# A fifth block product as seven small ones in the first channel product of an attention and MLP-mixer kernel

## The chip, the core and the metric

The kernel runs on one core of a Trainium2 chip. Its time is the device time of one execution, in microseconds (us). Three runs of the kernel before took 822.70, 823.24 and 823.75 us; the median is 823.24 us. The profiled execution took 823.35 us, of which the trace covers a span of 821.6 us.

## What is computed

A routed attention over 4 batches and 8 heads gives x of 768 tokens by 512 channels for each batch. A token mixer and a channel mixer follow. Cut to what matters here:

```
x  = attention(q, k, v, centroids)             # (4, 768, 512)
h  = relu(x^T @ w_tok1) @ w_tok2               # token mixer
u  = x + h^T
h2 = relu(u @ w_ch1) @ w_ch2                   # channel mixer: 512 -> 1536 -> 512
out = u + h2
```

The change lies in the product `u @ w_ch1`, called the first channel product.

## The kernel before

**Seven products for eight.** The channel products are done with the seven-product scheme of Strassen in Winograd's form. Both matrices are cut into 2 by 2 blocks. The left one is w_ch1 (blocks A11 to A22, sums S1 to S4, table `left_weights`), the right one is u transposed (blocks B11 to B22 of `uT`, sums T1 to T4, made by `u_sums`). Seven block products, named in the table `SEVEN`, give the four blocks of the result. VectorE (DVE) makes the sums of the operands and adds the products up; ScalarE (ACT) copies some of them out of PSUM and takes the relu.

**Parts.** The four batches are taken in the order 0, 2, 3, 1, and each is done in three parts, 12 in all. A part is one call of `ch1_pair`, which makes a third of the hidden rows (two chunks of 128, i = 0 and 1, by twice 384 tokens), and one call of `ch2_chunks`, which multiplies them by their third of w_ch2 and adds the result onto x. For `ch2_chunks` seven combinations of the hidden rows are needed; four of them, S1 to S4, are made by DVE at the end of `ch1_pair` (`sum_1`, `sum_2`, `sums_34`). `by_turns` runs the 21 items of `ch2_chunks`: the product p1 for chunks 0, 1, 2, then p5 for 0, 1, 2, then c11, and so on. Each item is two matmuls of 128x256 and one add by DVE, and after each item `between` takes one entry from the list `late` (ends of `ch1_pair` that wait their turn) and one from the list `others` (sums of operands for later parts).

**Sets.** In 11 of the 12 parts (all but the first) `ch1_sets` is used. There the scheme is applied a second time to four of the seven block products: Y (A12 by B21), P (S1 by T1), Z (S4 by B22) and X (A22 by T4). One block product is four matmuls of 128x384 (two chunks by two halves of the contraction); as a "set" it is seven of 128x192. The other three block products (A11 by B11, S2 by T2, S3 by T3) stay as they are, four matmuls of 128x384 each. The sums of the small blocks lie in the tiles `w1ss` (weights, made once) and `uTss` (u, made for each batch by `set_right_sums`).

**What sets the order.** The program is written out by hand: every engine executes its instructions in the order in which the code issues them, and waits are put in where an operand, or a buffer that is to be written over, isn't ready. PSUM has eight banks: three under the tag X, three under Z, and two under Y (`ptile`). A bank is given out again in turn, and the first matmul of its new user waits for the last reader of its old one. In `ch1_sets` the small products that are summed into one place run as a chain through a bank: p1, u2, c22, c21 in one accumulation (`chain`), with one add by DVE after each.

**Memory.** x of batch 1 is kept in the pool `x1pool` and is written to DRAM (the tile `spill`) after the first two batches' token mixers, so that its room can be used for the sums; it is read back into the room of batch 0 when that is done.

Of the kernel before, what the change touches and what calls it, by code (L numbers as in the profile page):

```python
# [18 lines left out]
C = 16  # L19
# [31 lines left out]
def kernel(  # L51
# [49 lines left out]
    tokpool = pool("tokpool", 1, tokens)  # L101
    staging = fast.enter_context(ExitStack())
# [30 lines left out]
    spill = spilled.tile([P, NJ, DM], F32, name="spill")  # L133
    xs = [(x1pool if b == 1 else xpool).tile([P, NJ, DM], F32, name=f"x{b}") for b in range(B)]
# [466 lines left out]

    def set_lefts():
        if "l2" not in pools:
            pools["l2"] = pools["w2sums"].tile([P, 4, 3, HS], F32, name="w1ss")
        l2 = pools["l2"]
        yx = W["ch1"].rearrange("p f (i r c) -> p f i r c", i=2, r=2)[:, 2:4]
        pz = pools["w1s"][:, 0:3:2].rearrange("p i f (r c) -> p f i r c", r=2)
        for n, both in enumerate((yx, pz)):
            blocks = [both[:, f, :, r] for r in range(2) for f in range(2)]
            sums_ = [l2[:, 2 * n : 2 * n + 2, m] for m in range(3)]  # L610
            yield dict(
                zip(("A11", "A12", "A21", "A22", "S1", "S2", "S4", "S3"), blocks + sums_ + blocks[2:3])
            )
# [6 lines left out]
    def set_rights():  # L620
        uT, R, r2 = pools["uT"], pools["R"], pools["r2"]
        yz = uT[:, :, 2:4].rearrange("p n f (k t) -> p n f k t", k=2)
        x, p = (R[name].rearrange("p f (k t) -> p f k t", k=2) for name in ("T4", "T1"))
        for blocks, sums_ in (
            ([yz[:, :, f, k] for f in range(2) for k in range(2)], [r2[:, 0:2, m] for m in range(3)]),
            ([x[:, f, k] for f in range(2) for k in range(2)], [r2[:, 2, m] for m in range(3)]),
            ([p[:, f, k] for f in range(2) for k in range(2)], [r2[:, 3, m] for m in range(3)]),
        ):
            yield dict(
                zip(("B11", "B12", "B21", "B22", "T1", "T2", "T4", "T3"), blocks + sums_ + blocks[1:2])  # L630
            )

    def set_right_sums():

        pools["r2"] = pools["w2sums"].tile([P, 4, 3, HS // 2], F32, name="uTss")
        return [list(winograd_right(blocks)) for blocks in set_rights()]

    def set_blocks():

        (yx, pz), (yz, x, p) = (list(y) for y in (set_lefts(), set_rights()))  # L640
        left = {name: {k: a[:, i] for k, a in two.items()} for two, i, name in
                ((yx, 0, "Y"), (yx, 1, "X"), (pz, 0, "P"), (pz, 1, "Z"))}
        right = {"Y": {k: b[:, 0] for k, b in yz.items()}, "Z": {k: b[:, 1] for k, b in yz.items()},
                 "X": x, "P": p}
        return left, right
# [94 lines left out]
    def between(n=1):  # L740
        if late:
            late.pop(0)()
        for _ in range(min(n, len(others))):
            others.pop(0)()

    def by_turns(n, product, of, last=False, after=()):
# [10 lines left out]
        for m in range(len(order) // 2):  # L757
# [9 lines left out]
            between()  # L767
# [16 lines left out]
    def ch1_pair(part, sets, beside):  # L784
# [6 lines left out]
        p5, c12 = (pools["mlp"].tile([P, 2, HS], F32, name=k) for k in ("p5", "c12"))  # L791
# [10 lines left out]

        def big(psum, a, r, i, start):
            product(psum, a, r, i, start)
            between()
            if a != "A11" and beside:
                beside.pop(0)()
# [13 lines left out]
        def sums_34():  # L821
            nc.vector.scalar_tensor_tensor(
                out=h2["S3"], in0=c12, scalar=0.0, in1=a11, op0=ALU.max, op1=ALU.subtract
            )
            sub(h2["S4"], a12, h2["S2"])

        (ch1_sets if sets else ch1_plain)(
            part, product, big, relu, a11, a12, a22, p5, c12, sum_1, sum_2, sums_34
        )

    def ch1_plain(part, product, big, relu, a11, a12, a22, p5, c12, sum_1, sum_2, sums_34):
# [24 lines left out]
        def late_(i):  # L856
            product(X[i], "A22", "T4", i, False)
            nc.scalar.activation(out=a12[:, i], in_=X[i], func=ACT.Relu)
            (sums_34 if i else sum_2)()
# [4 lines left out]
    def ch1_sets(part, product, big, relu, a11, a12, a22, p5, c12, sum_1, sum_2, sums_34):  # L864

        left, right = set_blocks()
        n0, n1 = slice(0, HS // 2), slice(HS // 2, HS)

# [7 lines left out]
        def direct(bank, which, start=True):  # L876
            small(bank[:, n0], which, "c11", start)
            small(bank[:, n1], which, "c12", start)

        def chain(q, which, name, x):  # L880

            small(q[:, n0], which, name, name == "p1")
            src = q[:, n0]
            if len(x.shape) == 3:
                src = src.unsqueeze(1).to_broadcast([P, 2, HS // 2])
            add(x, src, x)

        def column(z, which, x):
            small(z[:, n0], which, "p5")
            add(x[:, :, n1], z[:, n0].unsqueeze(1).to_broadcast([P, 2, HS // 2]), x[:, :, n1])  # L890

        X = [ptile("X", HS), None]
        big(X[0], "A11", "B11", 0, True)
        nc.scalar.copy(out=a11[:, 0], in_=X[0])  # L894
        ybe = ptile("Y", HS)
        direct(ybe, "Y")
        add(a11[:, 0], ybe, a11[:, 0])
        X[1] = ptile("X", HS)
        big(X[1], "A11", "B11", 1, True)
        nc.scalar.copy(out=a11[:, 1], in_=X[1])  # L900
        pbe = ptile("Z", HS)
        direct(pbe, "P")
        nc.scalar.copy(out=p5[:, 0], in_=pbe)
        yq, pq = ptile("Y", HS), ptile("Z", HS)
        chain(yq, "Y", "p1", a11[:, 0, n0])
        chain(pq, "P", "p1", p5[:, 0, n0])
        big(X[0], "S2", "T2", 0, False)
        chain(yq, "Y", "u2", a11[:, 0, n1])
        yz, pz = ptile("X", HS), ptile("Z", HS)
        column(yz, "Y", a11)  # L910
        chain(pq, "P", "u2", p5[:, 0, n1])
        small(pz[:, n0], "P", "p5")
        nc.scalar.copy(out=p5[:, 1, n1], in_=pz[:, n0])
        relu(a11[:, 0])
        add(p5[:, 0, n1], pz[:, n0], p5[:, 0, n1])
        add(c12[:, 0], X[0], p5[:, 0])
        big(X[1], "S2", "T2", 1, False)
        chain(yq, "Y", "c22", a11[:, 1, n1])
        chain(pq, "P", "c22", p5[:, 1, n1])
        direct(ybe, "Z")  # L920
        chain(yq, "Y", "c21", a11[:, 1, n0])
        small(pq[:, n0], "P", "c21", False)
        nc.scalar.copy(out=p5[:, 1, n0], in_=pq[:, n0])
        relu(a11[:, 1])
        add(c12[:, 0], ybe, c12[:, 0])
        chain(yz, "Z", "p1", c12[:, 0, n0])
        add(c12[:, 1], X[1], p5[:, 1])
        big(X[0], "S3", "T3", 0, False)
        add(a22[:, 0], X[0], p5[:, 0])
        relu(a22[:, 0])  # L930
        chain(yz, "Z", "u2", c12[:, 0, n1])
        column(pbe, "Z", c12)
        big(X[1], "S3", "T3", 1, False)
        add(a22[:, 1], X[1], p5[:, 1])
        relu(a22[:, 1])
        chain(yz, "Z", "c22", c12[:, 1, n1])
        direct(X[0], "X", False)
        nc.scalar.copy(out=a12[:, 0], in_=X[0])
        small(X[1][:, n0], "X", "c21", False)
        nc.scalar.copy(out=a12[:, 1], in_=X[1])  # L940
        chain(yz, "Z", "c21", c12[:, 1, n0])
        chain(yq, "X", "p1", a12[:, 0, n0])
        sum_1()

        def late_1():
            chain(yq, "X", "u2", a12[:, 0, n1])
            column(pz, "X", a12)
            sum_2()

        def late_2():  # L950
            chain(yq, "X", "c22", a12[:, 1].rearrange("p (k t) -> p k t", k=2))
            relu(a12)
            sums_34()

        late.extend([late_1, late_2])
# [166 lines left out]
    for b in (0, 2):  # L1122
# [26 lines left out]
        if b == 2:  # L1149
            take(turning, len(turning))  # L1150
            usums = u_sums()
            tok2_chunks(b, {13: lambda: next(usums)})
        else:
# [3 lines left out]
            nc.sync.dma_start(spill, xs[1])  # L1157
# [7 lines left out]
    batches = (0, 2, 3, 1)  # L1165
    for n, b in enumerate(batches):
        turning = []
        for part in range(3):
# [8 lines left out]
            ch1_pair(part, not first, [turning.pop(0) for _ in turning[:UCOLS]])  # L1177
# [25 lines left out]
            if part == 2 and not last:  # L1203

                yz, x, p = steps
                yz[0]()
                yz[1]()
                next(usums)

                others += [lambda: next(usums)] * 2  # L1210
                others.append(lambda: [step() for step in (yz[2], p[2], yz[3], p[3])])
                others += [lambda: None, lambda: (x[0](), x[1]()), lambda: (x[2](), x[3]())]
                if n == 0:
                    xs[1] = xpool.tile([P, NJ, DM], F32, name="x0")
                    nc.sync.dma_start(xs[1], spill)
# [216 lines left out]
```

## Time and profile before

| | value | where from |
|---|---|---|
| PE busy | 814.2 us, 99% of the span | part 1 of the page |
| DVE busy | 631.1 us, 77% | part 1 |
| ACT busy | 374.7 us, 46% | part 1 |
| PE's share of the chain that ended last | 98% | part 4 |
| granted TensorE clock | 1.00 | span and clock of the core |
| from the first matmul of the first part to that of the second | 393.51 to 429.75 us | timeline of PE |
| one part with sets, 535.69 to 571.00 us | PE busy 35.31, DVE 21.87, ACT 5.56 us | busy time by stretch |
| one matmul pair of 128x384, 128x256, 128x192 | 1.29, 0.86, 0.65 us | steps of the timeline of PE |

The page gives busy time for each engine and the chain of work that ended last. The trace can also be asked for the instructions of one engine in order of time (start, duration, line, tiles, and in brackets how long the engine was idle before and what ended that). In that timeline a matmul of this kernel leaves two records, so "x4" is two matmuls; the duration of a merged row runs to the end of its last record, while the next row starts earlier, as matmuls are pipelined. The step from one row's start to the next is therefore what a group of matmuls costs.

### The profile page before, as it was taken

The numbers are of one execution on the slowest core, as the hardware profiler recorded it, in microseconds if no ns is written. First come the engines' busy times: TensorE is split into PE (matmuls) and PEld (weight loads), VectorE is DVE, ScalarE is ACT, GpSimd is POOL, SyncE is SP. The second block draws the span as 40 slices with busy tenths as digits, with TensorE's granted clock in tenths as the row PEclk, the third lists the DMA queues.
The fourth block names the chain that finished last, engine by engine and source line by source line (L and its number), as shares of the span: only waits on it lengthen the run. The fifth ranks groups of instructions, "written<-read, shape, count | busy, mean of one in ns | idle before, by whom it ended". The sixth has DMA issues, their size and how long they took to land.

```text
span 821.6 us, 11693 instructions
## 1 busy us (share of the span) xinstructions
PE 814.2 (99%) x4348; PEld 535.5 (65%) x4348; DVE 631.1 (77%) x1206; ACT 374.7 (46%) x573; POOL 30.7 (4%) x28
## 2 busy tenths in 40 slices
PE   8999999999999999999999999999999999999997
PEld 4444444444444444444588888888888888888876
DVE  6879898989898978859797788755777566775665
ACT  5588776777878776127202154121441204511120
POOL 1001010111011000000000000000000000000000
PEclk9999999999999999999999999999999999999999
DMA  8797666768676434143000025000240001400002
GB/s 156 142 162 135 140 142 122 149 139 163 130 160 137 95 104 122 51 127 79 0 1 1 5 45 183 1 0 1 38 117 0 1 1 30 125 1 1 1 0 81
DMA packets 184258, 63.41 MB, mean 77 GB/s; under 512 B 172800, under 2 KB 176896, under 8 KB 183936
## 3 DMA queue, kind: packets, MB, share of 16 engines
q1 hardware_dynamic: 182592, 62.18, 34.7%
q8 instruction: 36, 0.59, 0.3%
q10 hardware_dynamic: 1600, 0.39, 0.2%
q14 instruction: 30, 0.25, 0.1%
HBM read 36.21 MB, written 7.86 MB: 54 GB/s over the span
## 4 chain that ended last, share of the span: by engine, by line
PE 98%; DVE 1%; issue 0%; ACT 0%; DVEq 0%; ACTq 0%
PE sc L413 19%; PE av L455 15%; PE pX L966 15%; PE pX L798 12%; PE pZ L966 7%; PE ph L534 5%; PE pY L871 5%; PE pZ L871 4%; PE pX L871 4%; PE pY L966 4%; PE pX L774 3%; PE small L491 2%; PE pZ L774 1%; PE small L304 1%; PE pZ L798 1%; PE pY L774 1%
## 5 line engine op out<-in xcount | busy, mean ns | idle before, releaser
L437 ACT ACTIVATE ex<-sc 128x768 f32<-128x768 f32 x192 | 151.0, 812 | 27.2 <-PE sc L413 15.5
L413 PE MATMUL sc<-qkT 64*128 64x384 f32 x768 | 155.3, 483 | 0.0
L445 DVE TENSOR_TENSOR sum<-sum,ex 128x768 f32<-128x768 f32 x128 | 127.8, 999 | 27.1 <-ACT ex L437 14.9
L455 PE MATMUL av<-ex,va 128*64 128x384 f32 x768 | 127.4, 488 | 0.0
L566 DVE TENSOR_TENSOR x<-pX,x 128x256 f32<-128x256 f32 (+1 forms) x168 | 75.8, 458 | 38.1 <-PE pX L966 37.6
L455 PEld LDWEIGHTS av<-ex,va 128*64 128x64 f32 x768 | 53.7, 137 | 71.7 <-issue 67.6
L413 PEld LDWEIGHTS sc<-qkT 64*128 64x128 f32 x768 | 67.8, 187 | 38.3 <-issue 38.0
L810 ACT ACTIVATE hA<-hA 128x384 f32<-128x384 f32 (+1 forms) x57 | 34.0, 597 | 85.4 <-DVE hA L566 85.1
L566 DVE TENSOR_TENSOR hA<-pY,hA 128x192 f32<-128x192 f32 (+1 forms) x90 | 36.7, 407 | 45.4 <-PE pY L871 42.7
L798 PE MATMUL pX<-uT,wc 128*128 128x384 f32 x192 | 69.8, 487 | 0.0
L894 ACT COPY hA<-pX 128x384 f32<-128x384 f32 x11 | 5.3, 479 | 131.3 <-PE pX L798 131.3
L413 PE MATMUL sc<-ohT 64*128 64x384 bf16 x384 | 62.4, 323 | 0.0
L462 ACT COPY avrows<-av 128x768 uint16<-128x768 uint16 x32 | 25.5, 797 | 44.4 <-PE av L455 44.4
L566 DVE TENSOR_TENSOR x<-pZ,x 128x256 f32<-128x256 f32 (+1 forms) x84 | 36.4, 455 | 11.4 <-PE pZ L966 11.3
L798 PEld LDWEIGHTS pX<-uT,wc 128*128 128x128 f32 x192 | 35.4, 190 | 14.7 <-issue 0.6
L534 PE MATMUL ph<-x,wt 128*128 128x512 f32 x96 | 41.6, 593 | 0.0
L413 PEld LDWEIGHTS <-ohT 64*128 64x128 bf16 x384 | 18.7, 94 | 33.8 <-issue 9.6
L966 PE MATMUL pX<-wc,hA 128*128 128x256 f32 x144 | 36.9, 380 | 0.3 <-ACT hA L940 0.3
L711 ACT COPY uT<-ucols 128x768 uint16<-128x768 uint16 x32 | 33.2, 1049 | 4.7 <-DMA ucols<-urows 4.7
L966 PE MATMUL pZ<-wc,hS 128*128 128x256 f32 x144 | 35.0, 379 | 0.0
L966 PE MATMUL pY<-wc,hA 128*128 128x256 f32 x144 | 35.0, 379 | 0.0
L798 PE MATMUL pX<-uTs,w1s 128*128 128x384 f32 x96 | 34.9, 486 | 0.0
(189 smaller groups left out, 1310.8 us busy)
## 6 DMA issues: line engine op xcount, KB each, us to landing
raw<-in_moe_w_ch_dram SPq DMA_DIRECT2D x24, 512.0 KB, 4.5
va<-in_v_dram SPq DMA_DIRECT2D x16, 384.0 KB, 3.7
out_dram<-x SPq DMA_DIRECT2D x24, 256.0 KB, 2.3
qk<-in_k_dram SPq DMA_DIRECT2D x60, 96.0 KB, 4.0
qk<-in_q_dram SPq DMA_DIRECT2D x60, 96.0 KB, 3.5
raw<-in_moe_w_tok_dram SPq DMA_DIRECT2D x3, 512.0 KB, 4.1
raw<-in_moe_w_tok_dram SPq DMA_DIRECT2D x4, 384.0 KB, 3.8
spill<-x SPq DMA_DIRECT2D x1, 1536.0 KB, 5.1
```

What stands on the lines that cost most here:

```text
L413: nc.tensor.matmul(sc[:, h, 0:HS], lhsT=src[rows, 1, j], rhs=src[rows, 0, HJ * qh : HJ * qh + HJ], start=start, stop=not start,)
L437: nc.scalar.activation(out=ex, in_=sc[:, :, 0:HS], func=ACT.Exp, scale=SM_SCALE)
L445: nc.vector.tensor_tensor(out=acc, in0=acc if j > 1 else st["ex", qh, 0], in1=st["ex", qh, j], op=ALU.add)
L455: nc.tensor.matmul(av[h * D : (h + 1) * D], lhsT=st["va"][:, h, j], rhs=ex[:, h], start=(j == 0), stop=(j == NJ - 1),)
L534: nc.tensor.matmul(pf, lhsT=W["tok1"][:, j, t * P : (t + 1) * P], rhs=xs[b][:, j], start=(j == 0), stop=(j == NJ - 1),)
L566: nc.vector.tensor_tensor(out=dst, in0=a, in1=b, op=ALU.add)
L711: nc.scalar.copy(out=out, in_=pools.pop(("ucols", i)).rearrange("p w j t -> p w (j t)"))
L774: nc.tensor.matmul(psum, lhsT=A[a][:, i], rhs=R[r], start=start, stop=True, skip_group_check=not start,)
L798: nc.tensor.matmul(psum, lhsT=A[a][:, k, c], rhs=R[r][:, k], start=start and k == 0, stop=k == 1, skip_group_check=not start,)
L810: nc.scalar.activation(out=x, in_=x, func=ACT.Relu)
L871: nc.tensor.matmul(psum, lhsT=left[which][a][:, part * P : part * P + P], rhs=right[which][r], start=start, stop=True, skip_group_check=no ...
L966: nc.tensor.matmul(psum, lhsT=h2[a][:, k, i * P : (i + 1) * P], rhs=Bw[w][:, part + 3 * k], start=start and k == 0, stop=k == 1, skip_grou ...
```

## The change

The block product S3 by T3 becomes a fifth set, U, so that in `ch1_sets` five block products are seven small matmuls each and two stay plain. What goes with it:

- U's result is no longer accumulated in the banks of the plain products. It is built up in a new tile `u3`, and the combinations are formed afterwards: `V` (a22 = bank + p5), `C` (c12 += a22), `B` (a22 += u3), `E` (a12 = bank + u3), each for both chunks.
- `w1ss` and `uTss` get a fifth slot for the sums of U's blocks: four more sums for each of three column parts of the weights, four more of u for each batch.
- The order of issue in `ch1_sets` is written anew as a list of names, `CH1`, and the eight banks are given out by the table `BANKS`. Its pieces after the first "|" are run one by one after the items of `ch2_chunks`, through `late`.
- The sums of u that are needed in the first part of a batch are no longer taken from `others`; they stand in the list where they are to be issued (`T2`, `yz0`, `x0`, `u0`, ...), as entries of `extra`.
- `between` takes from `others` only where `late` is empty, and `by_turns` spreads what is in `others` over the items that remain.
- For the room, x of batch 3 gets a place of its own (`x3pool`) and is spilled to DRAM as well, after its token mixer. Batch 3 is read back after batch 0 and batch 1 after batch 2.

```diff
-    spill = spilled.tile([P, NJ, DM], F32, name="spill")
-    xs = [(x1pool if b == 1 else xpool).tile([P, NJ, DM], F32, name=f"x{b}") for b in range(B)]
+    spill = {b: spilled.tile([P, NJ, DM], F32, name=f"spill{b}") for b in (1, 3)}
+    homes = (xpool, x1pool, xpool, x3pool)
+    xs = [homes[b].tile([P, NJ, DM], F32, name=f"x{b}") for b in range(B)]
...
         if late:
             late.pop(0)()
-        for _ in range(min(n, len(others))):
-            others.pop(0)()
+        else:
+            for _ in range(min(n, len(others))):
+                others.pop(0)()
...
-            between()
+            between(-(-len(others) // max(len(order) // 2 - m, 1)))
...
+    BANKS = {
+        "Zbe": 0, "Pbe": 0, "Uz": 0, "Ybe": 0, "Yq": 1, "Zq": 2, "X0": 3, "Pq": 4, "Ube": 5, "Pz":
+        5, "Zz": 5, "Yz": 5, "Xq": 5, "Uq": 6, "Xz": 6, "X1": 7,
+    }
+    CH1 = """
+        p1_0 yz0 T2 Zbe a11_0 Ya T3 Zc0 aside Za Pa Pbe +Za +Ya p2 Ube T4 Pc0 u2_0 Uc0 x0 x1 +Pa yz1
+        Pz Pd u0 Pcz Ua p3 Yd yz2 Uz +Pz Zd u1 Ucz Zz +Pd p1_1 yz3 Zcz +Ua u2 +Zz Pf +Yd +Zd a11_1
+        aside Ud u3 Yf +Uz Yz +Ud Ybe +Yf V0 Zf +Pf Uf +Ybe Yg +Yz Pg u2_1 x2 Pcg +Zf r11_0 +Yg +Uf
+        r11_1 C0 Zg Xbe B0 Zcg V1 Ug r22_0 C1 Xa Ucg E0 B1 x3 r22_1 aside +Xa
+        |
+        s1
+        |
+        Xz Xd Xg +Xd E1 +Xz s2
+        |
+        Xf +Xf r12
+        |
+        
+        |
+        
+        |
+        s4
+        |
+        
+        |
+        s3
+    """
+
+    def ch1_sets(part, product, relu, a11, a12, a22, p5, c12, s1, s2, s3, s4, u3, aside, extra):
         left, right = set_blocks()
         n0, n1 = slice(0, HS // 2), slice(HS // 2, HS)
+        bank = [ptile(tag, HS) for tag in "XXXZZZYY"]
...
+            do[f"V{i}"] = lambda: add(a22[:, i], X[i], p5[:, i])
+            do[f"C{i}"] = lambda: grow(c12[:, i], a22[:, i])
+            do[f"B{i}"] = lambda: grow(a22[:, i], u3[:, i])
+            do[f"E{i}"] = lambda: add(a12[:, i], X[i], u3[:, i])
...
             tok2_chunks(b, {13: lambda: next(usums)})
+            nc.sync.dma_start(spill[3], xs[3])
...
-                if n == 0:
-                    xs[1] = xpool.tile([P, NJ, DM], F32, name="x0")
-                    nc.sync.dma_start(xs[1], spill)
+                if n < 2:
+
+                    later = batches[n + 2]
+                    xs[later] = xpool.tile([P, NJ, DM], F32, name=f"x{b}")
+                    nc.sync.dma_start(xs[later], spill[later])
```

In the list a capital letter followed by a small one is a matmul: `Ya`, `Yd`, `Yf`, `Yg` are the chained p1, u2, c22, c21 of set Y, `Yz` its p5 and `Ybe` its c11 and c12. With a plus sign it is DVE's add of that product. `p1_i` and `u2_i` are the plain block products; `Zc0`, `Zcz`, `Zcg`, `a11_i` are copies and `r..` relus by ACT; `s1` to `s4` are DVE's sums of the hidden rows, 768 columns each.

More of the change, by code (lines that the diff above doesn't have):

```diff
@@ L101 @@
     tokpool = pool("tokpool", 1, tokens)
+    x3pool = pool("x3pool", 1, tokens)
     staging = fast.enter_context(ExitStack())
@@ L603, in set_lefts @@
         if "l2" not in pools:
-            pools["l2"] = pools["w2sums"].tile([P, 4, 3, HS], F32, name="w1ss")
+            pools["l2"] = pools["w2sums"].tile([P, 5, 3, HS], F32, name="w1ss")
         l2 = pools["l2"]
-        yx = W["ch1"].rearrange("p f (i r c) -> p f i r c", i=2, r=2)[:, 2:4]
+        w1 = W["ch1"].rearrange("p f (i r c) -> p f i r c", i=2, r=2)
         pz = pools["w1s"][:, 0:3:2].rearrange("p i f (r c) -> p f i r c", r=2)
-        for n, both in enumerate((yx, pz)):
+        for n, both in ((slice(0, 2), w1[:, 2:4]), (slice(2, 4), pz), (slice(4, 5), w1[:, 0:2, 1:2])):
             blocks = [both[:, f, :, r] for r in range(2) for f in range(2)]
-            sums_ = [l2[:, 2 * n : 2 * n + 2, m] for m in range(3)]
+            sums_ = [l2[:, n, m] for m in range(3)]
             yield dict(
@@ L622, in set_rights @@
         yz = uT[:, :, 2:4].rearrange("p n f (k t) -> p n f k t", k=2)
-        x, p = (R[name].rearrange("p f (k t) -> p f k t", k=2) for name in ("T4", "T1"))
+        x, p, u = (R[name].rearrange("p f (k t) -> p f k t", k=2) for name in ("T4", "T1", "T3"))
         for blocks, sums_ in (
@@ L627, in set_rights @@
             ([p[:, f, k] for f in range(2) for k in range(2)], [r2[:, 3, m] for m in range(3)]),
+            ([u[:, f, k] for f in range(2) for k in range(2)], [r2[:, 4, m] for m in range(3)]),
         ):
@@ L633, in set_right_sums @@
     def set_right_sums():
-        pools["r2"] = pools["w2sums"].tile([P, 4, 3, HS // 2], F32, name="uTss")
+        pools["r2"] = pools["w2sums"].tile([P, 5, 3, HS // 2], F32, name="uTss")
         return [list(winograd_right(blocks)) for blocks in set_rights()]
     def set_blocks():
-        (yx, pz), (yz, x, p) = (list(y) for y in (set_lefts(), set_rights()))
-        left = {name: {k: a[:, i] for k, a in two.items()} for two, i, name in
-                ((yx, 0, "Y"), (yx, 1, "X"), (pz, 0, "P"), (pz, 1, "Z"))}
+        (yx, pz, u), (yz, x, p, ur) = (list(y) for y in (set_lefts(), set_rights()))
+        left = {name: {k: a[:, i] for k, a in some.items()} for some, i, name in
+                ((yx, 0, "Y"), (yx, 1, "X"), (pz, 0, "P"), (pz, 1, "Z"), (u, 0, "U"))}
         right = {"Y": {k: b[:, 0] for k, b in yz.items()}, "Z": {k: b[:, 1] for k, b in yz.items()},
-                 "X": x, "P": p}
+                 "X": x, "P": p, "U": ur}
         return left, right
@@ L782, in tok2_chunks, with ch1_pair @@
         by_turns(DM, product, of, after=after)
-    def ch1_pair(part, sets, beside):
+    def ch1_pair(part, sets, beside, extra):
         h2 = pools["h2"] = {
@@ L790, in ch1_pair @@
         }
-        p5, c12 = (pools["mlp"].tile([P, 2, HS], F32, name=k) for k in ("p5", "c12"))
+        p5, u3, c12 = (pools["mlp"].tile([P, 2, HS], F32, name=k) for k in ("p5", "u3", "c12"))
         A, R = pools["A"], pools["R"]
@@ L801, in product, with aside @@
                 )
+        def aside():
+            if beside:
+                beside.pop(0)()
         def big(psum, a, r, i, start):
@@ L805, in big @@
             between()
-            if a != "A11" and beside:
-                beside.pop(0)()
+            if a != "A11":
+                aside()
         def relu(x):
@@ L819, in sum_2, with sum_3 @@
             sub(h2["S2"], h2["S1"], a11)
-        def sums_34():
+        def sum_3():
             nc.vector.scalar_tensor_tensor(
@@ L824, in sums_34, with sum_4, ch1_plain @@
             )
+        def sum_4():
             sub(h2["S4"], a12, h2["S2"])
[L827 to L831, printed above, removed]
+        if sets:
+            ch1_sets(part, product, relu, a11, a12, a22, p5, c12, sum_1, sum_2, sum_3, sum_4, u3, aside, extra)
+        else:
+            ch1_plain(part, product, big, relu, a11, a12, a22, p5, c12, sum_1, sum_2, sum_3, sum_4)
+        assert not beside
+    def ch1_plain(part, product, big, relu, a11, a12, a22, p5, c12, sum_1, sum_2, sum_3, sum_4):
         X, Z = {}, {}
@@ L858, in late_ @@
             nc.scalar.activation(out=a12[:, i], in_=X[i], func=ACT.Relu)
-            (sums_34 if i else sum_2)()
+            if i == 0:
+                sum_2()
+            else:
+                sum_3()
+                sum_4()
         late_(0)
         late.append(lambda: late_(1))
-    def ch1_sets(part, product, big, relu, a11, a12, a22, p5, c12, sum_1, sum_2, sums_34):
+    BANKS = {
[22 more added lines that the diff above has]
+    def ch1_sets(part, product, relu, a11, a12, a22, p5, c12, s1, s2, s3, s4, u3, aside, extra):
         left, right = set_blocks()
         n0, n1 = slice(0, HS // 2), slice(HS // 2, HS)
+        bank = [ptile(tag, HS) for tag in "XXXZZZYY"]
+        X = [bank[BANKS["X0"]], bank[BANKS["X1"]]]
+        target = {"Y": a11, "P": p5, "U": u3, "Z": c12, "X": a12}
+        copy = nc.scalar.copy
+        do = {"s1": s1, "s2": s2, "s3": s3, "s4": s4, "aside": aside, "r12": lambda: relu(a12)}
         def small(psum, which, name, start=True):
@@ L874, in small @@
             )
[L876 to L885, printed above, removed]
-            add(x, src, x)
-        def column(z, which, x):
-            small(z[:, n0], which, "p5")
-            add(x[:, :, n1], z[:, n0].unsqueeze(1).to_broadcast([P, 2, HS // 2]), x[:, :, n1])
@@ L892, in ch1_sets @@
[L892 to L955, printed above, removed]
+        def grow(x, src):
+            add(x, src, x)
+        def both(src):
+            return src.unsqueeze(1).to_broadcast([P, 2, HS // 2])
+        def names_of(which):
+            x = target[which]
+            q = bank[BANKS[which + "q"]][:, n0]
+            z = bank[BANKS[which + "z"]][:, n0]
+            be = X[0] if which == "X" else bank[BANKS[which + "be"]]
+            start = which != "X"
+            for name, what in (("a", "p1"), ("d", "u2"), ("f", "c22"), ("g", "c21")):
+                do[which + name] = lambda name=name, what=what: small(q, which, what, name == "a")
+            do[which + "z"] = lambda: small(z, which, "p5")
+            do[which + "be"] = lambda: (
+                small(be[:, n0], which, "c11", start), small(be[:, n1], which, "c12", start)
+            )
+            do[f"+{which}a"] = lambda: grow(x[:, 0, n0], q)
+            do[f"+{which}d"] = lambda: grow(x[:, 0, n1], q)
+            do[f"+{which}f"] = lambda: grow(x[:, 1, n1], q)
+            do[f"+{which}g"] = lambda: grow(x[:, 1, n0], q)
+            do[f"+{which}z"] = lambda: grow(x[:, 0, n1], z)
+            do[which + "c0"] = lambda: copy(out=x[:, 0], in_=be)
+            do[which + "cz"] = lambda: copy(out=x[:, 1, n1], in_=z)
+            do[which + "cg"] = lambda: copy(out=x[:, 1, n0], in_=q)
+            if which in "YX":
+                do[f"+{which}z"] = lambda: grow(x[:, :, n1], both(z))
+            if which == "Y":
+                do["+Ybe"] = lambda: grow(x[:, 0], be)
+            if which == "X":
+                do["+Xf"] = lambda: grow(x[:, 1].rearrange("p (k t) -> p k t", k=2), both(q))
+                do["Xg"] = lambda: small(X[1][:, n0], "X", "c21", False)
@@ new lines, in names_of_chunk @@
+        def names_of_chunk(i):
+            do[f"p1_{i}"] = lambda: product(X[i], "A11", "B11", i, True)
+            do[f"a11_{i}"] = lambda: copy(out=a11[:, i], in_=X[i])
+            do[f"u2_{i}"] = lambda: product(X[i], "S2", "T2", i, False)
+            do[f"V{i}"] = lambda: add(a22[:, i], X[i], p5[:, i])
+            do[f"C{i}"] = lambda: grow(c12[:, i], a22[:, i])
+            do[f"B{i}"] = lambda: grow(a22[:, i], u3[:, i])
+            do[f"E{i}"] = lambda: add(a12[:, i], X[i], u3[:, i])
+            do[f"r11_{i}"] = lambda: relu(a11[:, i])
+            do[f"r22_{i}"] = lambda: relu(a22[:, i])
@@ L957, in out_row, with issue @@
+        for which in target:
+            names_of(which)
+        for i in range(2):
+            names_of_chunk(i)
+        def issue(names):
+            for name in names.split():
+                if name in do:
+                    do[name]()
+                elif name in extra:
+                    extra.pop(name)()
+        first, *rest = CH1.split("|")
+        issue(first)
+        late.extend([lambda names=names: issue(names) for names in rest])
     def out_row(b, j):
@@ L1156 @@
             tok2_chunks(b)
-            nc.sync.dma_start(spill, xs[1])
+            nc.sync.dma_start(spill[1], xs[1])
             turning = list(u_steps(0))
@@ L1165 @@
     batches = (0, 2, 3, 1)
+    extra = {}
     for n, b in enumerate(batches):
@@ L1176 @@
                     others += steps
-            ch1_pair(part, not first, [turning.pop(0) for _ in turning[:UCOLS]])
+            ch1_pair(part, not first, [turning.pop(0) for _ in turning[:UCOLS]], extra)
+            assert not extra
             if first:
@@ L1203 @@
             if part == 2 and not last:
[L1205 to L1212, printed above, removed]
-                if n == 0:
-                    xs[1] = xpool.tile([P, NJ, DM], F32, name="x0")
-                    nc.sync.dma_start(xs[1], spill)
+                for name, sums_ in zip(("yz", "x", "p", "u"), steps):
+                    for m, step in enumerate(sums_):
+                        if name != "p" or m > 1:
+                            extra[f"{name}{m}"] = step
+                for m in (2, 3, 4):
+                    extra[f"T{m}"] = lambda: next(usums)
+                if n < 2:
+                    later = batches[n + 2]
+                    xs[later] = xpool.tile([P, NJ, DM], F32, name=f"x{b}")
+                    nc.sync.dma_start(xs[later], spill[later])
     def general():
```

## The prediction

> **What bounds the kernel now.** I read the page's busy times first, then the chain of waits.
>
> ```profile
> PE 814.2 (99%) x4348; PEld 535.5 (65%) x4348; DVE 631.1 (77%) x1206; ACT 374.7 (46%) x573; POOL 30.7 (4%) x28
> ...
> PE 98%; DVE 1%; issue 0%; ACT 0%; DVEq 0%; ACTq 0%
> ```
>
> PE is the bound from end to end, so every us of matmul taken out counts if no new wait appears, and every wait of PE counts in full. Three rows of part 5 (all parts of the kernel) give the matmuls' cost only roughly; the timeline of PE gives the step: in the part from 535.69 us, two matmuls of 128x384 advance it by 1.29 us (0.646 each), two of 128x192 by 0.65 (0.325), two of 128x256 by 0.86 (0.432). Cost goes by columns: 192 costs half of 384, nothing more.
>
> The next question is how near to a wait PE runs. The list of PE's waits shows only 0.3 us after 550 us. But the steps in the timeline show more. In the first part of each later batch there is a small one:
>
> ```profile
> 620.33 0.49 PE L871 MATMUL pX<-uTs,w1ss 128*128 128x192 f32 x2
> 620.86 0.59 PE L871 MATMUL pX<-uTss,wc 128*128 128x192 f32 x2
> 621.29 0.49 PE L871 MATMUL pX<-uTss,w1s 128*128 128x192 f32 x2
> ```
>
> The first step is 0.53, the next 0.43, where 0.325 is due: 0.205 of waiting and 0.105 of getting going again, 0.31 in all. On DVE at that time:
>
> ```profile
> 620.25 0.55 DVE L566 TENSOR_TENSOR hA<-pX,p 128x384 f32<-128x384 f32 x1
> ```
>
> This add reads the bank that the matmul at 620.86 writes. It ends at 620.80; PE starts 0.06 later. So a full DVE queue does hold PE through a bank, and these are its prices: DVE's end plus 0.06, then 0.10 to restart.
>
> Last, DVE's queue at the end of an ordinary part:
>
> ```profile
> 551.43 0.36 DVE L566 TENSOR_TENSOR c<-pX,c 128x192 f32<-128x192 f32 x1 [0.80 <-PE pX L871]
> 551.82 0.36 DVE L566 TENSOR_TENSOR hA<-pY,hA 128x192 f32<-128x192 f32 x1
> 552.10 0.95 DVE L814 SCALAR_TENSOR_TENSOR hS<-c,hA 128x768 f32<-128x768 f32 x1
> 552.96 0.42 DVE L566 TENSOR_TENSOR x<-pX,x 128x256 f32<-128x256 f32 x1
> 553.30 0.35 DVE L566 TENSOR_TENSOR hA<-pY,hA 128x192 f32<-128x192 f32 x1
> 553.78 0.56 DVE L566 TENSOR_TENSOR hA<-pZ,hA 128x384 f32<-128x384 f32 x1
> 554.25 0.95 DVE L563 TENSOR_TENSOR hS<-hS,hA 128x768 f32<-128x768 f32 x1
> 555.12 0.42 DVE L566 TENSOR_TENSOR x<-pX,x 128x256 f32<-128x256 f32 x1
> ```
>
> DVE was idle for 0.80 us just before 551.43, and is full from there to 558 us. The steps are DVE's prices: 0.28 us for 192 columns, 0.34 for 256, 0.47 for 384, 0.87 for 768. They are not quite all: ten steps from 551.82 to 557.85 should make 5.66 and make 6.03; eleven from 616.28 to 620.72 should make 4.03 and make 4.44. Both have 0.037 per instruction on top[...]. The third p5 item (pZ) starts at 556.85 (555.12 + 4 x 0.432); its bank's last reader, the add at 553.78, ends at 554.34. That is 2.5 us of slack now.
>
> [...]
>
> **The change, part by part.** (1) *PE work.* S3 by T3 loses 4 x 0.646 = 2.58 us and gains 7 x 0.325 = 2.28: 0.31 less per part, 11 parts, **-3.4 us**. LDWEIGHTS go from 40 to 43 per part; they are beside the matmuls, and at 128x192 already keep up.
>
> (2) *DVE work per part.* Before, 14 adds of 192, 10 of 384, 4 sums of 768. After, from the list: 18, 12 and 4. That is 4 x 0.28 + 2 x 0.47 = 2.1 us more, where a part of 35.3 us has DVE busy for 21.9. On average it fits. What matters is where it lies.
>
> (3) *The new order at the end of a part.* In the table of banks, Xq (the chain Xa, Xd, Xf) is bank 5, the third Z bank. The third p5 item takes the third Z bank, so it waits for the add +Xf. In DVE's queue +Xf now stands behind S1 and S2. Count both engines from the start of the product Ud. PE, to the third p5: 18 small products (5.85), u2_1 (1.29), five items of 128x256 (4.32) = **11.46 us**. DVE: +Ud can start 0.53 after Ud starts (as 539.57 to 540.10 us for such a pair before). From it to +Xf there are 8 adds of 192 (2.24), 11 of 384 (5.17), 3 of 256 (1.02), S1 and S2 (1.74) = 10.17; then +Xf to its end, 0.56; then 0.06. Plain sum: 0.53 + 10.17 + 0.56 + 0.06 = 11.32, no wait. With 0.037 for each of 24 instructions (0.89): 12.21, a wait of 0.75. These are the bounds of an unknown. Counted singly (three adds read what the one before wrote: +Yz, B0, +Xz, 0.14 each, as 0.65 instead of 0.47 at 616.28 shows with a margin[...]) it is 0.81: a wait of 0.67. I take this, plus 0.10 for the restart: 0.77 in each of 11 parts, **+8.5 us**. Behind the waiting pZ stands the whole of `ch2_chunks`, and nothing later gives the time back, as PE has no idle time in which to catch up.
>
> (4) *First part of batches 2, 3, 1.* The sums x2 and x3 of u stand behind +Ud as well: 0.56 more in the same queue, so Xd and Xf (same bank 5, each waiting for the add before it) wait too. The four new sums u0 to u3 (1.1 us) come just ahead. I take 0.56 of waiting and two restarts (0.2) beyond (3), and one early wait of about 0.15; the 0.31 seen above is in the old order and goes. +0.6 each, **+1.8 us**.
>
> (5) *First batch.* `others` gets eight more sums (four of u, 0.28 each, four of weights, about as much) and is emptied faster, in the item loop after the first part, where DVE is full from 410.7 to about 428 us now; the backlog reaches the next part, whose Zc0 by ACT waits for a bank behind it. At least 0, at most the 2.2 us of work; I take **+0.9**.
>
> (6) *Spill of batch 3.* It starts after its last add (392.1 us now) and took 5.1 us for batch 1. `w1ss` lies over the place of x3, so its first sum waits; that one ran at 401.35, 4 us after the landing. Nothing. Reading back: 7.0 us, with two batches' parts (over 100 us) before use. Nothing. ACT (16% busy in a part): two more copies of 0.48 and 0.32 per part; nothing, except as they sit in the chain of (3), counted there.
>
> Sum: -3.4 + 8.5 + 1.8 + 0.9 = +7.8; 823.24 + 7.8 = **831.0 us**.
>
> **Rivals.** (A) *The queue just keeps up* (plain sum of (3), 0.14 of slack, and so little in (4) and (5)): only the 3.4 is left, 819.8 us. For it: 77% DVE on average, and 0.9 us decides. Against: both full stretches before show the 0.037. (B) *Half of it*: a wait of 0.25 with restart 0.35 per part (3.9), (4) and (5) at 0.2 together: 823.9, no change. (C) *Worse*: the wait shifts DVE's later sums S3 and S4, or the weights' sums pile up, and more items wait: another 0.5 per part, 836.5. For it: DVE is full to the end of S4; against: the S3 and S4 users come a dozen items later. (D) *A transfer*: `w1ss` waits for the spill. It would need over 4 us of delay, and cost some 3 more once: 834.
>
> **Chances.** Forecast 0.68, A 0.10, B 0.07, C 0.09, D 0.06. The range runs from a wait of 0.35 instead of 0.67 in (3) with (4) and (5) kept (827) to just under C: 826.5 to 834.5. Faster by over 0.2% only in A and a little of B: 0.11; within 0.2%: 0.05; slower: 0.84.
>
> **What would show it.** PE's busy time without waits falls by about 3.4 us; in each part with sets the third p5 item starts 0.6 to 0.9 us late, and DVE's +Xf ends 0.06 before it; DVE shows no idle time between +Ud and +Xf. The first item of the list of PE's waits should be the 128x256 matmul into pZ, released by DVE's add. I am wrong if that step is 0.43 as for the others: then the time is near 820. I am also wrong if PE waits mainly elsewhere in the list, for example at the copies by ACT that free p5, c12 and u3.

## The result, and the profile after

The changed kernel takes **828.35 us** (median of 6 runs, 828.18 to 828.81), the kernel before on the same chip 823.5 (6 runs, 822.7 to 823.75). The ratio is 1.0061, with a 95% interval of 1.0048 to 1.0074: a little slower, by 4.9 us.

Busy time and the engines' shares of the chain that ended last, in the page of the changed kernel:

```profile
PE 815.4 (99%) x4414; PEld 541.7 (66%) x4414; DVE 654.7 (79%) x1300; ACT 389.7 (47%) x617; POOL 30.7 (4%) x28
...
PE 87%; DVE 10%; issue 2%; ACT 0%; DVEq 0%; ACTq 0%
```

PE still shows 99%, as before, and 1.2 us more of busy time, although there is less to multiply. Busy time says little here: the end of a group of matmuls is modelled, and an idle moment is partly covered (of the 0.44 us shown below, 0.28 counts as idle). The second line says more. Before, the chain stood on PE for 98% of the span; now it leaves PE again and again for DVE, 10% in all. The list of PE's waits says where (tile, line, releaser: total us, number, mean us):

```profile
PE pZ L1000 <- DVE hA L568: 3.7, 11, 0.4
...
PE pZ L923 <- DVE hA L568: 0.4, 1, 0.4
PE pX L923 <- ACT c L951: 0.4, 1, 0.4
```

The first row is eleven waits of the 128x256 matmul into pZ, one for each part with sets. It was not there before: from the first channel product on, the list of the kernel before has this row alone.

```profile
PE pX L966 <- ACT hA L940: 0.3, 1, 0.3
```

The place in PE's timeline, in an ordinary part (not a batch's first, and not the last of all), before and after. Before, all three items of p5 are one row, and the next row starts 2.59 us later, which is six times 0.432, so PE waits for nothing:

```profile
555.12 2.75 PE L966 MATMUL pZ<-w2s,hS 128*128 128x256 f32 x12
557.71 1.89 PE L966 MATMUL pY<-wc,hA 128*128 128x256 f32 x8
```

After:

```profile
556.95 1.89 PE L1000 MATMUL pZ<-w2s,hS 128*128 128x256 f32 x8
559.12 1.13 PE L1000 MATMUL pZ<-w2s,hS 128*128 128x256 f32 x4 [0.28 <-DVE hA L568]
560.09 0.61 PE L1000 MATMUL pY<-wc,hA 128*128 128x256 f32 x2
```

The eight records at 556.95 are four matmuls, the first two items of p5: four times 0.432 is 1.73 us, and they take 2.17. So the third p5 item is 0.44 late. (The bracket says 0.28 because it counts from the modelled end of the matmul before.) The third item itself, two matmuls, takes 0.97 where 0.864 is due: 0.105 to get going again.

What DVE did from the product `Ud` on. PE's row of that product first, then DVE's, from `+Ud` to `+Xf`:

```profile
547.22 0.49 PE L923 MATMUL pY<-uTss,w1ss 128*128 128x192 f32 x2
```

```profile
547.75 0.36 DVE L568 TENSOR_TENSOR u<-pY,u 128x192 f32<-128x192 f32 x1 [0.44 <-PE pY L923]
...
552.06 0.55 DVE L568 TENSOR_TENSOR hA<-pY,p 128x384 f32<-128x384 f32 x1
552.71 0.56 DVE L568 TENSOR_TENSOR c<-hA,c 128x384 f32<-128x384 f32 x1
...
557.32 0.95 DVE L565 TENSOR_TENSOR hS<-hS,hA 128x768 f32<-128x768 f32 x1
558.18 0.42 DVE L568 TENSOR_TENSOR x<-pX,x 128x256 f32<-128x256 f32 x1
558.52 0.55 DVE L568 TENSOR_TENSOR hA<-pZ,hA 128x384 f32<-128x384 f32 x1
558.98 0.74 DVE L568 TENSOR_TENSOR x<-pZ,x 128x256 f32<-128x256 f32 x2
```

`+Ud` starts 0.53 after the product, and no row of DVE between it and `+Xf` has a bracket: the longest gap is the 0.10 us before 552.71. The row at 557.32 is S2, the one at 558.52 `+Xf`. It ends at 559.07 and PE starts at 559.12. By its own steps PE would have been at the place 11.46 us after 547.22, at 558.68.

### The profile page after: what moved, and what is told of

It reads as the page before. It is cut to its first block, busy times and chain, and to the rows that moved or that the text cites. A ratio compares the mean times of both kernels' runs of the same rounds, so it can differ in the third digit from the quotient of the medians.

```text
span 826.5 us, 11970 instructions
## 1 busy us (share of the span) xinstructions
PE 815.4 (99%) x4414; PEld 541.7 (66%) x4414; DVE 654.7 (79%) x1300; ACT 389.7 (47%) x617; POOL 30.7 (4%) x28
## 4 chain that ended last, share of the span: by engine, by line
PE 87%; DVE 10%; issue 2%; ACT 0%; DVEq 0%; ACTq 0%
PE sc L415 19%; PE av L457 15%; PE pX L1000 11%; PE pX L923 6%; PE pZ L1000 5%; PE ph L536 5%; PE pZ L923 4%; DVE hA L568 4%; PE pZ L803 4%; PE pY L1000 4%; PE pY L803 3%; PE pX L779 2%; DVE x L568 2%; PE small L493 2%; PE pY L923 1%
## 5 line engine op out<-in xcount | busy, mean ns | idle before, releaser
L965 ACT COPY hA<-pZ 128x384 f32<-128x384 f32 x11 | 5.3, 478 | 126.1 <-PE pZ L803 111.1
L1000 PE MATMUL pZ<-w2s,hS 128*128 128x256 f32 x144 | 36.0, 387 | 3.7 <-DVE hA L568 3.7
L1000 PE MATMUL pX<-wc,hA 128*128 128x256 f32 x144 | 35.0, 379 | 0.0
L536 PEld LDWEIGHTS ph<-x,wt 128*128 128x128 f32 x96 | 18.2, 190 | 23.1 <-issue 22.6
L1000 PE MATMUL pX<-w2s,hA 128*128 128x256 f32 x144 | 33.2, 379 | 0.0
L1000 PE MATMUL pX<-wc,hS 128*128 128x256 f32 x144 | 33.2, 379 | 0.0
```

The source lines that it names most:

```text
L536: nc.tensor.matmul(pf, lhsT=W["tok1"][:, j, t * P : (t + 1) * P], rhs=xs[b][:, j], start=(j == 0), stop=(j == NJ - 1),)
L1000: nc.tensor.matmul(psum, lhsT=h2[a][:, k, i * P : (i + 1) * P], rhs=Bw[w][:, part + 3 * k], start=start and k == 0, stop=k == 1, skip_grou ...
```

## The experiments

All are whole kernels on the same chip as the runs of before beside them. I kept the theory of the prediction (DVE's queue holds a bank in every part with sets; the rest is small) and set three rivals against it: that the larger amount of work on DVE costs the time wherever it lies, that the spill of batch 3 takes part in it, and that the sums in the first parts of the batches are the main loss.

### S2 behind the add that frees the bank

Changed kernel, one word of the list moved:

```diff
-        Xz Xd Xg +Xd E1 +Xz s2
+        Xz Xd Xg +Xd E1 +Xz
         |
-        Xf +Xf r12
+        Xf +Xf r12 s2
```

> Only the sum S2 moves, from ahead of the add +Xf to behind it; the work of every engine is the same as in the changed kernel. Theory (the third p5 item waits for +Xf, which stands 0.87 us too late behind S2): the waits of 0.44 to 0.57 us and their restarts of 0.10 go in all 11 parts, 6.6 us in all, so about 821.7 us. Rival 1 (what costs is the 2.1 us of DVE work that each part has more, wherever it stands): 828.3 us as before the move. Rival 2 (PE waits for something else, such as ACT's copies or the spill): 828.3 us too.

Measured: **821.2 us**, ratio to before 0.9977 (0.9969 to 0.9986). Against the changed kernel's ratio of 1.0061 this is about 7 us less, so that the change is now a small gain. The row of eleven waits is gone from the list. DVE's timeline, and PE's at the same place:

```profile
555.10 0.55 DVE L568 TENSOR_TENSOR hA<-pZ,hA 128x384 f32<-128x384 f32 x1
555.56 0.95 DVE L565 TENSOR_TENSOR hS<-hS,hA 128x768 f32<-128x768 f32 x1
```

```profile
554.40 2.75 PE L1000 MATMUL pZ<-w2s,hS 128*128 128x256 f32 x12
556.99 1.89 PE L1000 MATMUL pY<-wc,hA 128*128 128x256 f32 x8
```

`+Xf` comes first, then S2; PE's twelve records are the six matmuls of all three p5 items in one row, and take 2.59 us, six times 0.432. DVE's work is the same as in the changed kernel:

```profile
PE 811.9 (99%) x4414; PEld 543.2 (66%) x4414; DVE 654.4 (80%) x1300; ACT 390.0 (48%) x617; POOL 30.7 (4%) x28
```

654.4 us against 654.7. So the amount of work on DVE isn't what costs these 7 us; its place in the queue is.

### S3 ahead of it as well

The opposite: one more long sum in front of `+Xf`, again with the work unchanged.

```diff
-        Xz Xd Xg +Xd E1 +Xz s2
+        Xz Xd Xg +Xd E1 +Xz s2 s3
...
-        s3
+        
```

> The other way round: the sum S3 (768 columns, 0.87 us in DVE's queue) also goes ahead of +Xf, right behind S2; nothing else moves. Theory: each of the 11 waits grows by the 0.87 us that now stands in front, 9.6 us in all, so about 838 us, and the third p5 item waits 1.3 us in an ordinary part. Rival 1 (amount of DVE work): unchanged, 828.3 us. Rival 2: unchanged.

Measured: **837.52 us**, ratio 1.0174 (1.0158 to 1.0190), 9.2 us more than the changed kernel. PE's waits, DVE's queue and PE's timeline:

```profile
PE pZ L1000 <- DVE hA L568: 13.2, 11, 1.3
```

```profile
559.69 0.95 DVE L565 TENSOR_TENSOR hS<-hS,hA 128x768 f32<-128x768 f32 x1
560.56 0.95 DVE L831 SCALAR_TENSOR_TENSOR hS<-c,hA 128x768 f32<-128x768 f32 x1
561.43 0.42 DVE L568 TENSOR_TENSOR x<-pX,x 128x256 f32<-128x256 f32 x1
561.76 0.55 DVE L568 TENSOR_TENSOR hA<-pZ,hA 128x384 f32<-128x384 f32 x1
```

```profile
559.33 1.89 PE L1000 MATMUL pZ<-w2s,hS 128*128 128x256 f32 x8
562.36 1.13 PE L1000 MATMUL pZ<-w2s,hS 128*128 128x256 f32 x4 [1.14 <-DVE hA L568]
```

The third p5 item is 3.03 - 1.73 = 1.30 late, instead of 0.44. The step from S3 to the next row is 0.87 us, and the wait has grown by 0.86. One us put ahead of that add is one us lost in each part: no slack is left to take it up, and PE doesn't catch up later.

### The spill alone, in the kernel before

Kernel before, with nothing of the change but the place and the spill of batch 3 and the new order of reading back:

```diff
+    x3pool = pool("x3pool", 1, tokens)
...
-    spill = spilled.tile([P, NJ, DM], F32, name="spill")
-    xs = [(x1pool if b == 1 else xpool).tile([P, NJ, DM], F32, name=f"x{b}") for b in range(B)]
+    spill = {b: spilled.tile([P, NJ, DM], F32, name=f"spill{b}") for b in (1, 3)}
+    homes = (xpool, x1pool, xpool, x3pool)
+    xs = [homes[b].tile([P, NJ, DM], F32, name=f"x{b}") for b in range(B)]
...
+            nc.sync.dma_start(spill[3], xs[3])
...
-                if n == 0:
-                    xs[1] = xpool.tile([P, NJ, DM], F32, name="x0")
-                    nc.sync.dma_start(xs[1], spill)
+                if n < 2:
+                    later = batches[n + 2]
+                    xs[later] = xpool.tile([P, NJ, DM], F32, name=f"x{b}")
+                    nc.sync.dma_start(xs[later], spill[later])
```

> The kernel before with one part of the change alone: batch 3 in a place of its own, spilled after its token mixer and read back after batch 0, batch 1 after batch 2. Theory (the transfers are hidden): 823.5 us, no difference beyond 0.1%. Rival (the sums that lie over the spilled tile wait for its landing, or the 3 MB more of traffic hold up the transposes): 825 to 827 us, with a wait in the first part.

Measured: 823.26 us, ratio **1.0001** (0.9993 to 1.0009). The spill costs nothing that can be measured (the interval leaves room for 0.7 us). Why it can't be felt in the changed kernel is seen in its DMA rows (count, KB each, median us from issue to landing) and in its timeline, where the first sum that is written over the place of x3 comes long after the issue:

```profile
spill<-x SPq DMA_DIRECT2D x2, 1536.0 KB, 5.1
x<-spill SPq DMA_DIRECT2D x2, 1536.0 KB, 6.4
```

```profile
392.14 0.33 SPq L1187 DMA_DIRECT2D spill<-x  x1
```

```profile
401.33 0.42 DVE L568 TENSOR_TENSOR w1ss<-wc 128x256 f32<-128x256 f32 x1
```

Issue at 392.14 plus 5.1 is 397.2, some 4 us before 401.33. That sum ran at 401.35 in the kernel before.

### Sums of u a little earlier

The first experiment's kernel, and three of the sums that a batch's first part needs taken into the last three items of the part before it:

```diff
                 after[17] = lambda: (steps[2][0](), steps[2][1]())
+                after[18] = lambda: next(usums)
+                after[19] = lambda: steps[0][0]()
+                after[20] = lambda: steps[0][1]()
...
-                        if name != "p" or m > 1:
+                        if (name != "p" or m > 1) and (name != "yz" or m > 1):
...
-                for m in (2, 3, 4):
+                for m in (3, 4):
```

> As e1, and three sums of u for the next batch (T2 and the first two of Y and Z) stand in the last three items of the batch before, where DVE has idle time between its adds, instead of in the list of the first part. Theory: beyond e1 some of the waits early in the three first parts go, 0.3 us each, so 820.9 us or about 0.9 below e1, and clearly below the kernel before. Rival (the waits of the first parts come from the end of the list, where x2 and x3 stand, alone): as e1, 821.7 us.

Measured: 820.61 us, ratio 0.9971 (0.9961 to 0.9982). The medians are 0.6 us apart from the first experiment's, and the steps of PE that are longer than due add up to 3.3 us instead of 3.9; the intervals overlap, so the ratios don't tell the theory from its rival. The traces do show the early waits shrink: one in each of the three first parts, 0.15 to 0.16 us in the first experiment, is 0.05 here. The first parts of the batches do hold a loss, but a small one.

### The other edit of the item loop, taken back

Changed kernel, but only one entry of `others` is taken after each item, as before:

```diff
-            between(-(-len(others) // max(len(order) // 2 - m, 1)))
+            between()
```

> The changed kernel with one edit undone: by_turns takes one entry of the list of operand sums after each item, as before, not as many as spread them over the items left. Theory (the sums that don't get their turn are made in one go at the end of the first part, DVE's queue is then 2 to 3 us late, and the second part's first products wait for it): one wait of 2.5 to 3 us there instead of the 0.6 us of the changed kernel, less 0.9 us of waits that go at the start of the third part, so about 830 us (829.5 to 831). Rival (PE has enough banks to run over it): unchanged, 828.3 us.

Measured: **831.87 us**, ratio 1.0106 (1.0091 to 1.0122), some 3.5 us more than the changed kernel, and 0.9 above the range that was expected. One row among PE's waits has changed by more than 0.1 us, at the start of the second part of the first batch:

```profile
PE pX L923 <- ACT c L951: 2.9, 1, 2.9
```

DVE's queue shows what was in the way. The sums that had not been taken in the loop are done in one go behind it. Behind them stand six small checks of values (`fits`), and the copy by ACT, which frees the bank, waits for the last of these (two rows of DVE from a stretch without a pause, and the copy):

```profile
431.28 0.69 DVE L565 TENSOR_TENSOR w2s<-wc 128x512 f32<-128x512 f32 x1
...
435.13 0.17 DVE L1031 TENSOR_REDUCE good<-inside 128x1 f32<-128x16 f32 x1
```

```profile
435.38 0.48 ACT L951 COPY c<-pX 128x384 f32<-128x384 f32 x1 [3.43 <-DVE good L1031]
```

That a copy waits for checks it has nothing to do with is seen in the kernel: `fits` puts its flags (`inside`) into the room of the tile c12 (`tag="c12"`), and c12 is what the copy writes.

In the changed kernel the same queue is done at 432.55, and the wait is the 0.4 of its list. So this edit earns its keep: it spreads the backlog of the first batch. Of the 3.5 us the longer wait is 2.5: by the steps PE is 3.06 late here instead of 0.53. The rest is taken up in the last section.

### The small checks of the first batch moved to the second

The kernel of the fourth experiment, and one number changed: the six small operations of DVE behind the first part (`fits`), and the small matmul and one copy by DVE behind the second (`fits_count`), are issued a batch later, when DVE has less to do.

```diff
-            if n == 0 and part < 2:
+            if n == 1 and part < 2:
```

> As e4, and the seven small DVE instructions that check the range of the values (lines of fits and fits_count) run in the second batch instead of at the end of the first part and after the second. Theory (they stand in DVE's queue ahead of the first add of the second part, whose bank the plain product waits for through ACT): the wait of 0.6 us there goes, so 0.5 to 0.6 us below e4, 820.0 us. Rival (the wait there comes from the sums of the weights alone): as e4, 820.6 us.

Measured: **819.9 us**, ratio 0.9965 (0.9951 to 0.9978). The row of the wait for ACT is gone from the list; for pX at that line it has only this one, for DVE's add:

```profile
PE pX L923 <- DVE x L568: 0.3, 1, 0.3
```

By the ratios it is 0.5 us below the fourth experiment, but the intervals overlap, so I don't call the step shown. PE's steps say that part of it comes back elsewhere: the wait of 0.53 at the start of the second part is gone, but one of 0.50 stands at the start of the third, where it was 0.24. Against both the kernel before and the changed one the version is faster: 3.1 us below its runs of before (823.0), and by the ratios about 8 us below the changed kernel.

## Why the prediction was right

The direction was right, 828.35 lies in the range, and 831.0 was 2.65 us too high. By its own steps (lateness is taken from the starts of PE's records from 393 us on: what each step is longer than the matmuls of its kind need):

| step | predicted, us | measured, us | from |
|---|---|---|---|
| (1) PE work | -3.4 | -3.5 | what remains, span less lateness: 821.6 - 2.3 = 819.3 before, 826.5 - 10.7 = 815.8 after |
| (3) third p5 item | +8.5 | +6.6 | eleven waits, 5.5 together, and eleven restarts of 0.104 |
| (4) first parts of batches 2, 3, 1 | +1.8 | +0.9 | 1.93 late after, 1.06 before |
| (5) first batch | +0.9 | +0.8 | 1.45 late after, 0.63 before |
| (6) spill | 0 | 0 | the third experiment |
| last part | none | +0.1 | a wait for DVE's `+Xd`, 0.60, where before one for a copy by ACT took 0.49 |
| sum | +7.8 | +4.9 | 828.35 - 823.5 |

**What held.** Three of the signs that the prediction named are there: the row of 11 waits into pZ heads PE's list; `+Xf` ends 0.05 to 0.06 before PE starts; and DVE shows no idle time from `+Ud` to `+Xf`, in nine of the eleven parts (the third part of the first batch has one of 0.46, the last part one of 0.81). The restart costs 0.10, as step (3) took it. The weight loads kept up: one takes 0.19 us where a matmul of 128x192 advances PE by 0.325. One sign was not met: the third p5 item should have been 0.6 to 0.9 late, and is 0.44 late in six parts and 0.56 in five. The first two experiments show the cause both ways: with S2's 0.87 us taken out of the queue ahead of `+Xf` all eleven waits go, with S3's 0.87 put in each grows by 0.86 to 0.87. Step (2), that DVE's extra work is free in itself, is shown by the first experiment for the ordinary parts; in the first parts and the first batch that kernel still waits longer than the kernel before, 3.9 us in all against 2.3. The whole loss rests on the order in DVE's queue, and the trace shows it: `+Xf` had its product since about 557.2 us, stood behind S2 and started at 558.52. The first experiment delays S2 without a new wait.

**What was mis-sized.** The term that failed most is DVE's overhead in (3): I put 0.81 us on top of the sum of steps for 24 instructions, and it was 0.60. From `+Ud` to `+Xf` the trace has 10.77 us (547.75 to 558.52), where I had 10.17 + 0.81 = 10.98. The starts in DVE's queue show where the 0.60 stands. Four adds that take up what the add just before them wrote or read (`+Yz`, `B0`, `C1`, `+Xz`) start 0.11, 0.11, 0.18 and 0.11 later than the plain prices say; `C1` is the row at 552.71 above, 0.65 after the one before it instead of 0.47. `+Yf` adds 0.11 and S1 0.06, and the other 18 steps come out 0.1 shorter together, as the prices were rounded. So the prediction's 0.42 for three such adds is 0.33, the 0.18 of `C1` it lacked, and of the other 0.39, my estimate with no trace behind it, only about 0.08 is there (`+Yf` and S1, less the rounding). An ordinary part therefore waits for 0.44, not 0.67. Five parts, in which PE had already waited a little earlier, wait for about 0.56, and the mean of the eleven is 0.50. The miss of 0.17 comes eleven times: it is 1.9 of the 2.9 us.

Most of the remainder is (4): I let `x2` and `x3` hold PE for 0.56 and two restarts beside the wait of (3). The trace has the p5 wait 0.12 longer there and 0.29 of new lateness in each of the three first parts. Which of these sums causes which wait I didn't separate by a run.

**What was luck.** (5) came out at +0.8, near the +0.9, but from other pieces. At the place that I named, the copy by ACT at the start of the second part, PE loses 0.64 with the restart. Two waits in the third part, 0.35 and 0.23 with theirs, I had not foreseen, and one of the kernel before, 0.40, is gone.

**One reading that was off.** The changed kernel has four more copies of 192 columns by ACT in a part, not two copies of 0.48 and 0.32; nothing in the sum hung on it.

**The rivals.** A (the queue just keeps up) is out by the eleven waits; but 0.44 us in a queue of 11 decided between its 819.8 and 828.4, and the first experiment, with no such wait left, comes to 821.2. B asked for waits of 0.25 in (3): the 0.44 of an ordinary part lies between that and my 0.67, and no nearer to mine. B is out by its time, 823.9. C (more items wait) is out: no other row of `ch2_chunks` is in PE's list. D is out by the third experiment.

**What stays open.** The first experiment gains 6.9 us by the ratios and by PE's lateness, and 7.4 by the spans (826.5 to 819.1), where the waits and restarts of (3) make 6.6. Of the spans' surplus 0.4 us has nothing to do with the edit: the first channel product starts at 393.49 in one trace and at 393.10 in the other. Another 0.2 is a wait in the third part of the first batch (at 485.18) that went too.

## What to carry to other kernels

Where one engine is busy for 99% and another empties its banks, the second engine's average doesn't tell whether the first will wait (here 79% with eleven waits, 80% with none of them): count both queues from the last event that they share to the last reader of each bank that comes round again. Put a long sum that nobody needs soon behind the add that frees the next bank; here moving one word in a list was worth 7 us and turned a loss of 0.6% into a gain of 0.2%. When the margin is under one us in a queue of eleven, give both signs a real chance and try the order both ways, since a few tenths of a us of overhead in the whole queue decide.

## What the runs showed of the hardware

**A wait costs more than itself.** After every wait of 0.1 us or more that PE had in the two channel products of the changed kernel, the first item took 0.10 us longer than due (above, 0.97 instead of 0.864 for two matmuls). It was the same whether it had been late by 0.44, by 1.30 or by 3 us (the last two in the second and fifth experiments). Even where PE was late by 0.01 us only, at 615.74 in the changed kernel, the next row starts 0.43 later instead of 0.325. Eleven short waits thus lose 1.1 us beyond their length.

**After a wait of some 3 us the clock fell.** In the fifth experiment, after the long wait, PE's timeline and the table by stretches (us; busy time and count of PE, PEld, DVE, ACT, POOL; granted clock; DMA share; GB/s) show:

```profile
435.92 0.59 PE L923 MATMUL pX<-uTs,w1s 128*128 128x192 f32 x2 [2.90 <-ACT c L951]
...
437.77 2.69 PE L803 MATMUL pZ<-uTs,w1s 128*128 128x384 f32 x4
```

```profile
436.00:438.00 2.00, 2.00 (x9) 2.00 (x10) 0.88 (x3) 0.48 (x1) 0.00 (x0) 0.71 0.00 0
438.00:440.00 2.00, 2.00 (x4) 1.09 (x4) 0.00 (x0) 0.48 (x1) 0.00 (x0) 0.50 0.00 0
440.00:442.00 2.00, 2.00 (x12) 1.73 (x12) 0.72 (x3) 0.32 (x1) 0.00 (x0) 0.94 0.00 0
```

Two matmuls of 128x384 take 2.53 us (437.77 to 440.30) where 1.29 is due. Worked out from the clocks of the three stretches, with 0.5 as the low value, the granted clock is 1.00 until about 0.9 us after PE is back at work, then 0.5 for 3.4 us, then 1.00 again. By PE's rows this loses about 1.7 us; with the 2.5 of the wait, less some 0.7 of waits in the third part that this order doesn't have, it makes the 3.5 us.

The wait before it was 2.90 us by the bracket and 3.06 by the step. The mean clock was 0.997 in all four executions of this kernel, and 0.998 to 1.00 in those of all the others. Among these is the second experiment, in which PE's list has eleven waits into pZ, 1.3 us at the longest, with a mean clock of 0.999 to 1.00. What decides whether the clock falls isn't shown by these runs.
